# Retention attention into a routed MLP: where the sums, the weights and the placing of the early pair stand in the queues

## Chip, cores and metric

The kernel runs on one core of one Trainium2 chip. The metric is the time of one execution on the device in microseconds; the number compared is the median of several executions. All data are float32 unless said otherwise.

## The reference

An attention block without softmax (a retention: 4 batches, 8 heads, 768 positions, head width 64) gives 3072 rows of 512 numbers. Each row then goes through one of 8 experts, the one with the largest logit, and is scaled by its softmax probability.

```
state = gamma * state + k[t] (x) v[t];  y[t] = scale * q[t] @ state        # per batch and head
x = y of all heads side by side                                            # 3072 x 512
logits = x @ w_gate;  e = argmax(logits);  gate = softmax(logits)[e]
out[row] = gate * (relu(x[row] @ w1[e]) @ w2[e])                           # w1: 512 x 1024, w2: 1024 x 512
```

## The kernel before, in words

**Attention.** The work is cut into 12 steps (`STEPS`), each of two tiles of 128 rows. Step s computes the scores of a block of positions, the part that comes from the running state, the new state and the outputs (`scores`, `with_state`, `next_state`, `within`). One step later, `to_rows` turns the outputs into rows on VectorE and `store` writes them to a buffer in device memory, `x_d`, by four DMAs on SyncE's queue; `logits` and `logits_of` give the gate logits.

**Routing while attention runs.** Rows are sorted to experts in three portions (`NEXT` = 0, 5, 9, 12), by the generator `place(i)`. Each `next(rest)` issues its next piece: softmax parts and the chosen expert, then the ranks (small matmuls `rk`, then VectorE up to `here`), then `found` (a matmul), then the addition to `inv` (line 705), the table from which rows are fetched and written back. `WHEN` and `step` (764 to 768) say in which step and at which of five places ("p", "a", "b", "r", "c") a piece is issued. At the end of portion 1, GpSimd gathers the first 256 rows of expert 0 and of expert 1 from `x_d` by indirect DMAs (the early rows). Portion 2, of the last six tiles, is placed after the steps.

**The early pair.** Expert 0's first 256 rows, two tiles of 128, are computed before the other rows are known. In the last step ScalarE copies them (`xe`), TensorE transposes them (`early_rows`), and the loop at 840 runs the first layer over 8 f-blocks of 128 (`layer1`, `hTa`), with the pieces of portion 2 between the blocks. The second layer of the pair is done in `pair` by Winograd's scheme with seven products of half matrices in place of eight. It needs four sums of w2's quarters (`halves_of_w`, tiles `we`) and four of `hTa`'s (`halves_of_h`, tiles `he`). The products come in the order A11 B11; S2 T2; S3 T3; S1 T1; A12 B21; A22 T4; S4 B22. Between them stand VectorE's parts (`part`, line 361) and 16 transposes of expert 0's other rows into `xTa` (`spare`).

**Sums and queues.** Before, VectorE makes sums 0 and 1 of w2, sums 0 and 1 of h and sum 3 of w2; GpSimd makes sum 2 of w2 and sums 2 and 3 of h. `arms` (line 429) works out from the row counts which of 33 code variants each expert takes, and `regs` (414) loads that number into registers of TensorE and ScalarE. `sources`, `gates_of` and `targets` (179 to 208) are short chains of VectorE operations on `inv`: where rows come from, their gate and where they go. The late gathers of 128-row tiles 2 and 3 of both experts follow `sources`.

**Weights.** `weights1` and `weights2` issue DMAs on SyncE's queue, in program order with the stores. Expert 0's w1 comes in step 9 in two halves; half of its w2 (1 MB) is asked for after the store of step 10's rows, the other half after that of step 11's.

**After the pair.** Jobs of the 8 experts follow, with 512 rows at most each; job 0 does what is left of expert 0 and begins at once with `layer1` on `xTa`.

**Order.** From line 739 on, the order on all five engines is that of the program text (`manual_schedule`); nothing is reordered. An instruction that waits holds up all behind it on its engine or queue.

Of the kernel before, what the change touches and what calls it, by code (L numbers as in the profile page):

```python
# [13 lines left out]
F32 = mybir.dt.float32  # L14
# [4 lines left out]
ALU = mybir.AluOpType  # L19
AX = mybir.AxisListType  # L20

P = 128
# [31 lines left out]
def kernel(  # L54
# [11 lines left out]
    nc = tc.nc  # L66
# [87 lines left out]
            nc.sync.dma_start(w1t[:, :, :, part], w1v[:, ds(e, 1), :, part])  # L154
        return w1t

    def weights2(pool, e, part=range(FT), w2t=None):
        if w2t is None:
            w2t = pool.tile([P, 1, FT, DM], F32, tag="w2t", name="w2t")
        part = slice(part.start, part.stop)  # L160
        nc.sync.dma_start(w2t[:, :, part, :], w2v[:, ds(e, 1), part, :])
        return w2t

    def weights(pool, e):
# [86 lines left out]

    FH, DH = FT // 2, DM // 2

    def halves_of_h(hT, hs, others=nc.vector):


        hs = [h.rearrange("p (f t) -> p f t", f=FH) for h in hs]
        a11, a12, a21, a22 = (hT[:, ts(j, FH), ts(i, P)] for i in range(2) for j in range(2))
        nc.vector.tensor_tensor(out=hs[0], in0=a21, in1=a22, op=ALU.add)
        nc.vector.tensor_tensor(out=hs[1], in0=hs[0], in1=a11, op=ALU.subtract)  # L260
        others.tensor_tensor(out=hs[2], in0=a11, in1=a21, op=ALU.subtract)
        others.tensor_tensor(out=hs[3], in0=a12, in1=hs[1], op=ALU.subtract)
        return hs

    def halves_of_w(w2t, ws, which=range(4), by=nc.vector):
# [176 lines left out]
    with ExitStack() as actx:  # L442
# [145 lines left out]
        def store(s):  # L588
            m, b1, e = where[s]
            xg = x.pop(("g", s))  # L590
            for g in range(Q):
                nc.sync.dma_start(x_d[ts((2 * m + e) * 2 + b1, 2 * P), ts(g, P)].rearrange("(t l) r -> l t r", l=L),
                                  xg[ts(g, L), :, :, :].rearrange("p b q r -> p (b q) r"))
# [14 lines left out]
        def logits_of(s, lgT, bank):  # L608
            tr = bank[:, 2 * P : 4 * P].rearrange("p (b t) -> p b t", b=2)
            for b in range(2):  # L610
                nc.tensor.transpose(tr[:, b, :], lgT[:, ts(b, P)], ident)
            return lambda: nc.vector.tensor_reduce(
                lg[:, 2 * s : 2 * s + 2, :], tr.rearrange("p b (a e) -> p b e a", a=DT)[:, :, 0:E, :], axis=AX.X,
                op=ALU.add)
# [146 lines left out]
                copy(out=xTa[:, :, ts(t, P)], in_=tr)  # L761

        rest = iter(())
        WHEN = {5: "abc", 6: "ab", 7: "ab", 8: "pp", 9: "ar", 10: "pp"}

        def step(s, at):
            for _ in range(WHEN.get(s, "").count(at)):
                next(rest, None)

        for s in range(STEPS):  # L770
            if s + 3 < STEPS:
                if s % 2:
                    load_all("q", s + 3)
                load_all("k", s + 3)
                load_all("v", s + 3)
            if s % 2 and s + 1 < STEPS:
                scale_q(s + 1, 1)
            if s + 1 < STEPS:
                for b in range(2):
                    scale_v(s + 1, b)  # L780
            if s % 2 == 0 and s + 2 < STEPS:
                scale_q(s + 2, 0)
            if s in (1, 2):
                nc.gpsimd.memset(xs2[s % 2], 0.0)
            if s:
                am = [scores(s, b) for b in range(2)]
            y = outputs()
            if s + 1 == STEPS:
                logit = logits(s - 1)
            if where[s][0] or where[s][2]:  # L790
                with_state(s, y)

            def ahead():
                for b in range(2):
                    turn_k(s + 1, b)

            def ahead_q():
                if s % 2:
                    for b in range(2):
                        turn_q(s + 1, b)  # L800

            step(s, "p")
            if s:
                if s + 1 < STEPS:
                    logit = logits(s - 1)
                    ahead()
                if s + 1 == STEPS:
                    for t in range(HALF):
                        nc.scalar.copy(out=xe[:, t, :].rearrange("p (a q l) -> p q a l", q=Q, l=L),
                                       in_=xs2[0][:, t, :].rearrange("p (q a l) -> p q a l", q=Q, l=L))  # L810
                reduce = logits_of(s - 1, *logit)
                if s + 1 < STEPS:
                    ahead_q()
                to_rows(s - 1)
                reduce()
                store(s - 1)
                if s == NEXT[NR - 1]:
                    wa = [weights1(first, 0, 2)]
                if s + 1 == STEPS:
                    wa.append(weights2(first, 0, range(FT // 2)))  # L820
                if s in NEXT:
                    rest = chain(rest, place(NEXT.index(s) - 1))
                step(s, "a")
            next_state(s)
            step(s, "b")
            if s == NEXT[NR - 1] + 1:
                pad_ranks(acc[:, NR - 1, 0:2])
            step(s, "r")
            within(s, y, am, early_rows if s + 1 == STEPS else lambda: None)
            if s == 0:  # L830
                ahead()
            step(s, "c")

        rest = place(NR - 1)
        oa = xs2[0][:, 0:HALF, :]
        we = [att.tile([P, FH * DH], F32, tag=tag, name="we", bufs=bufs)
# [3 lines left out]
        for f in range(FT):  # L840
            layer1(EARLY, xTa, wa[0], hTa, f, (("sc", 4),))
            if f == 0:
                logit = logits(STEPS - 1)
            if f == 1:
                logits_of(STEPS - 1, *logit)()
                next(rest)
                to_rows(STEPS - 1)
                store(STEPS - 1)
                weights2(first, 0, range(FT // 2, FT), wa[1])
            if f == 3:  # L850
                next(rest)
            if f == 4:
                ne = count()
            if f == 6:
                next(rest)
                next(rest, None)
        src, far = sources(inv, "")
        for e in range(2):
            gather(xs2[e], src[:, ts(e, TC)], range(HALF, TC))
        egates, gates = gates_of(early[0], "_e"), gates_of(inv, "")  # L860
        arm, over = arms(ne)
        dst = targets(inv, far, "")
        halves_of_w(wa[1], we, [0, 1])
        halves_of_w(wa[1], we, [2], nc.gpsimd)
        S = halves_of_h(hTa, [att.tile([P, FH * P], F32, tag="k", name="he", bufs=8) for _ in range(4)], nc.gpsimd)
        T = halves_of_w(wa[1], we, [3])
        which = regs(0)

        late = turns(xs2[0], xTa, range(HALF, TC))

        def some(n):
            for _ in range(n):
# [2 lines left out]
        pair(hTa, wa[1], S, T, oa, egates, lambda: fetch_ahead(which, 0),  # L875
             lambda name: att.tile([P, FH * P], F32, tag="v", name=name, bufs=8)[:, 0:DH], some,
             (("sc", 4), ("sc", 4), ("y", 2), ("y", 2)))
        scatter(oa, targets(*early, "_e"), range(HALF))
        turn(xs2[1], xT1, range(TC))
        cols = [(src[:, ts(e, TC)], dst[:, ts(e, TC)], gates[:, ts(e, TC)]) for e in range(E)]  # L880

        cols[0] = (None, dst[:, HALF:TC], gates[:, HALF:TC])
# [204 lines left out]
```

## Time and profile before

| What | us |
|---|---|
| median of 3 runs | 462.06 |
| the runs | 461.9 to 463.61 |
| the profiled execution | 460.4 |
| its span on the chip | 458.7 |
| busy TensorE (PE) | 432.3 |
| busy VectorE (DVE) | 278.8 |
| busy GpSimd (POOL) | 249.1 |
| busy ScalarE (ACT) | 126.1 |
| mean granted TensorE clock | 0.985 |

The profiled execution is one run; its span is what the instructions on the chip cover, and the 1.7 us between the two lie around it. Places in the span are given in microseconds from its start. Attention's steps run to about 119, the first layer of the early pair to about 135, its second layer to about 157, and the jobs of the experts to 450. In the page, PE is a matmul and PEld the load of its weights, which overlaps; SPq is SyncE's queue of DMAs. A line number such as L271 is that of the kernel, and of a helper where one issues the instruction. "<-" names who ended a wait.

### The profile page before, as it was taken

What the parts mean: (1) busy time and instruction counts of PE and PEld (TensorE: products, weight loads), DVE (VectorE), ACT (ScalarE), POOL (GpSimd) and SP (SyncE); (2) the same over time, 40 slices, a digit from 0 to 9 for tenths busy, and PEclk for the clock granted to TensorE, in tenths of its full rate; (3) what the DMA queues carried; (4) which work ended last, traced back from release to release, by engine and by line L of the source; (5) the groups of instructions that cost most, each with busy time, mean ns of one, the idle gap of its engine ahead of it and who ended that gap; (6) DMA issues with size and microseconds to landing.
All of it is one profiled execution on the core that took longest, in us unless ns stands there. A gap on an engine that the chain in (4) does not pass through costs nothing.

```text
span 458.7 us, 9508 instructions
## 1 busy us (share of the span) xinstructions
PE 432.3 (94%) x3595; PEld 352.8 (77%) x3595; DVE 278.8 (61%) x583; ACT 126.1 (27%) x286; POOL 249.1 (54%) x203
## 2 busy tenths in 40 slices
PE   7799999988985999999999999999999999999992
PEld 4688888876764855669968995897897699699772
DVE  4444689696377984643775677267666848744410
ACT  3355355343410111120231131124132112202310
POOL 4575535445026058548906890984589099089211
PEclk9999999999995999999999999999999999999998
DMA  9999999999750099425614713281481524001001
GB/s 201 234 236 211 238 242 215 236 203 301 228 156 25 25 378 385 164 98 199 213 33 160 258 72 137 78 299 36 159 260 58 186 92 172 6 6 64 4 29 50
DMA packets 94471, 72.75 MB, mean 159 GB/s; under 512 B 53898, under 2 KB 78474, under 8 KB 94352
## 3 DMA queue, kind: packets, MB, share of 16 engines
q1 hardware_dynamic: 89088, 58.74, 46.5%
q0 software_dynamic: 5120, 12.60, 7.6%
q8 instruction: 47, 0.77, 0.7%
q14 instruction: 72, 0.59, 0.4%
q10 hardware_dynamic: 144, 0.05, 0.0%
HBM read 60.88 MB, written 14.68 MB: 165 GB/s over the span
## 4 chain that ended last, share of the span: by engine, by line
PE 82%; DVE 7%; SPq 4%; DMA 3%; issue 2%; ACT 1%; POOL 0%; POOLq 0%; DVEq 0%; ACTq 0%
PE p L309 24%; PE p L355 18%; PE p L242 15%; PE p L229 6%; PE sc L523 3%; PE y L574 3%; PE hp L229 3%; SPq L472 2%; PE new L556 2%; PE trk L491 2%; PE y L543 2%; PE trq L491 2%; DMA xs<-x_d,src_e 1%; DMA k<-in_k_dram 1%; DVE xTa L215 1%
## 5 line engine op out<-in xcount | busy, mean ns | idle before, releaser
L242 PE MATMUL p<-w2t,hT 128*8 128x128 f32 (+6 forms) x496 | 67.3, 362 | 0.1
L242 PEld LDWEIGHTS p<-w2t,hT 128*8 128x8 f32 (+6 forms) x496 | 32.1, 122 | 31.0 <-issue 26.7
L215 DVE STREAM_TRANSPOSE xT<-xs 32x512 f32<-32x512 f32 x64 | 44.9, 702 | 6.2 <-issue 5.0
L400 POOL DMA_INDIRECT out_dram<-o,dst x30 | 29.8, 993 | 28.6 <-ACT o L250 12.1
L525 DVE TENSOR_TENSOR am<-sc,causal 128x512 f32<-128x512 f32 x48 | 30.1, 684 | 22.4 <-PE sc L523 20.8
L485 POOL TENSOR_TENSOR vs<-v,dec 128x512 f32<-128x512 f32 x23 | 23.6, 1043 | 32.0 <-DMA v<-in_v_dram 26.9
L215 DVE STREAM_TRANSPOSE xTs<-xs 32x512 f32<-32x512 f32 x48 | 33.7, 702 | 11.6 <-DMA xs<-x_d,src 7.5
L1046 POOL COPY turn_of<-t 128x1 f32<-128x1 f32 x6 | 1.1, 183 | 71.7 <-DVE t L295 71.7
L172 POOL DMA_INDIRECT xs<-x_d,src x28 | 28.3, 1012 | 18.8 <-issue 7.9
L355 PE MATMUL p<-ws,hs 128*128 128x256 f32 x168 | 37.4, 379 | 0.0
L309 PE MATMUL p<-t,w1t 128*128 128x196 f32 (+5 forms) x192 | 35.9, 330 | 0.3 <-DVE q L313 0.3
L309 PE MATMUL p<-t,s 128*128 128x196 f32 (+5 forms) x192 | 35.8, 329 | 0.0
L313 DVE TENSOR_TENSOR hT<-p,q 128x196 f32<-128x196 f32 (+5 forms) x72 | 23.8, 359 | 19.0 <-PE p L309 16.5
L355 PEld LDWEIGHTS p<-ws,hs 128*128 128x128 f32 x168 | 31.9, 190 | 4.3
L271 POOL TENSOR_TENSOR ws<-w2t,ws 128x1024 f32<-128x1024 f32 x14 | 33.0, 2357 | 0.6
L271 POOL TENSOR_TENSOR ws<-w2t 128x1024 f32<-128x1024 f32 x14 | 33.1, 2362 | 0.1
L309 PEld LDWEIGHTS p<-t,w1t 128*128 128x128 f32 x192 | 32.4, 190 | 0.7 <-DVE q L313 0.7
L309 PEld LDWEIGHTS p<-t,s 128*128 128x128 f32 x192 | 32.4, 190 | 0.0
L480 POOL TENSOR_TENSOR qs<-q,dec 128x512 f32<-128x512 f32 x22 | 22.3, 1042 | 17.2 <-DMA q<-in_q_dram 17.2
L361 DVE SCALAR_TENSOR_TENSOR o<-p,gate,q 128x256 f32<-128x256 f32 x21 | 10.1, 483 | 31.0 <-PE p L355 23.7
L313 DVE TENSOR_TENSOR q<-p,q 128x196 f32<-128x196 f32 (+5 forms) x48 | 16.4, 360 | 18.0 <-PE p L309 12.3
L523 PE MATMUL sc<-qT,kT 64*128 64x128 f32 x384 | 24.9, 279 | 2.3 <-ACT kT L510 2.3
(208 smaller groups left out, 825.8 us busy)
## 6 DMA issues: line engine op xcount, KB each, us to landing
w1t<-in_moe_w_dram SPq DMA_DIRECT2D x7, 2048.0 KB, 8.3
w2t<-in_moe_w_dram SPq DMA_DIRECT2D x7, 2048.0 KB, 10.5
k<-in_k_dram SPq DMA_DIRECT2D x24, 256.0 KB, 6.0
v<-in_v_dram SPq DMA_DIRECT2D x24, 256.0 KB, 5.4
x_d<-xg SPq DMA_DIRECT2D x48, 128.0 KB, 4.0
q<-in_q_dram SPq DMA_DIRECT2D x11, 512.0 KB, 6.1
w1t<-in_moe_w_dram SPq DMA_DIRECT2D x2, 1024.0 KB
w2t<-in_moe_w_dram SPq DMA_DIRECT2D x2, 1024.0 KB
```

Of the source, the lines that this page charges most:

```text
L172: nc.gpsimd.indirect_dma_start(out=xs[:, t, :], out_offset=None, in_=x_d[0:rows, :], in_offset=bass.IndirectOffsetOnAxis(ap=idx[:, t : t + ...
L215: nc.vector.transpose(xT[ts(g, L), :, 0 : n * P].rearrange("p a (t r i) -> p r t a i", r=Q, i=L)[:, r, :, :, :], xs[ts(r, L), tiles[0] : t ...
L229: nc.tensor.matmul(hp, lhsT=w1t[:, 0, dt, ts(f, P)], rhs=xT[:, dt, 0:n], start=(dt == 0), stop=(dt == DT - 1))
L242: nc.tensor.matmul(y[j * z : j * z + m, 0:c], lhsT=hT[:, f, t * P + r0 : t * P + r0 + m], rhs=w2t[:, 0, f, ts(j, c)], start=(i == 0), stop ...
L271: by.tensor_tensor(out=ws[i], in0=sums[i][0], in1=sums[i][1], op=ALU.subtract)
L309: nc.tensor.matmul(rows(y), lhsT=a(d, f), rhs=b(d), start=start and d == 0, stop=d == 1, skip_group_check=True)
L313: nc.vector.tensor_tensor(out=to, in0=rows(y), in1=rows(plus), op=ALU.add)
L355: nc.tensor.matmul(y, lhsT=a[:, f, :], rhs=b[:, f, :], start=start and f == 0, stop=f == FH - 1, skip_group_check=True)
L400: done = nc.gpsimd.indirect_dma_start(out=out[:, :], out_offset=bass.IndirectOffsetOnAxis(ap=idx[:, t : t + 1], axis=0), in_=o[:, t, :], i ...
L485: by.tensor_tensor(out=vs, in0=raw.pop(("v", s, b)), op=ALU.mult, in1=inner(dec[:, ts(NC + 2 * where[s][0] + where[s][2], H)], D))
L523: nc.tensor.matmul(sc[j][:, a, :], lhsT=kT[r, a, :], rhs=qT[r, a, :], start=True, stop=True)
L525: nc.vector.tensor_tensor(out=am[j], in0=sc[j], in1=middle(causal[:, :], HP), op=ALU.mult)
```

## The change

`halves_of_h` takes a list of sums in place of an engine, and all eight sums of the early pair are issued on VectorE, in the order w 0, w 1, h 0, h 1, w 2, h 2, w 3, h 3. Both halves of expert 0's w2 are asked for in the last step ahead of the store of step 10's rows. `arms` moves from behind the loop to f-block 4; the last pieces of portion 2, with `sources`, the late gathers and the gates of all rows, move from f-block 6 and behind the loop to f-block 5; `regs(0)` moves to f-block 6. The gates and targets of the early rows are worked out ahead of the loop, the targets of all rows behind the transposes of expert 1's rows. In the steps, place "p" moves from ahead of the logits to behind them and the key transposes (this concerns steps 8 and 10), and the ranks of portion 1 in step 9 move from place "r", ahead of `within`, to "c", behind it.

```diff
--- before.py
+++ after.py
@@ -154,11 +154,10 @@
             nc.sync.dma_start(w1t[:, :, :, part], w1v[:, ds(e, 1), :, part])
         return w1t
 
-    def weights2(pool, e, part=range(FT), w2t=None):
-        if w2t is None:
-            w2t = pool.tile([P, 1, FT, DM], F32, tag="w2t", name="w2t")
-        part = slice(part.start, part.stop)
-        nc.sync.dma_start(w2t[:, :, part, :], w2v[:, ds(e, 1), part, :])
+    def weights2(pool, e, parts=1):
+        w2t = pool.tile([P, 1, FT, DM], F32, tag="w2t", name="w2t")
+        for part in (ts(i, FT // parts) for i in range(parts)):
+            nc.sync.dma_start(w2t[:, :, part, :], w2v[:, ds(e, 1), part, :])
         return w2t
 
     def weights(pool, e):
@@ -251,15 +250,14 @@
 
     FH, DH = FT // 2, DM // 2
 
-    def halves_of_h(hT, hs, others=nc.vector):
+    def halves_of_h(hT, hs, which=range(4)):
 
 
         hs = [h.rearrange("p (f t) -> p f t", f=FH) for h in hs]
         a11, a12, a21, a22 = (hT[:, ts(j, FH), ts(i, P)] for i in range(2) for j in range(2))
-        nc.vector.tensor_tensor(out=hs[0], in0=a21, in1=a22, op=ALU.add)
-        nc.vector.tensor_tensor(out=hs[1], in0=hs[0], in1=a11, op=ALU.subtract)
-        others.tensor_tensor(out=hs[2], in0=a11, in1=a21, op=ALU.subtract)
-        others.tensor_tensor(out=hs[3], in0=a12, in1=hs[1], op=ALU.subtract)
+        sums = (a21, a22, ALU.add), (hs[0], a11, ALU.subtract), (a11, a21, ALU.subtract), (a12, hs[1], ALU.subtract)
+        for i in which:
+            nc.vector.tensor_tensor(out=hs[i], in0=sums[i][0], in1=sums[i][1], op=sums[i][2])
         return hs
 
     def halves_of_w(w2t, ws, which=range(4), by=nc.vector):
@@ -761,7 +759,7 @@
                 copy(out=xTa[:, :, ts(t, P)], in_=tr)
 
         rest = iter(())
-        WHEN = {5: "abc", 6: "ab", 7: "ab", 8: "pp", 9: "ar", 10: "pp"}
+        WHEN = {5: "abc", 6: "ab", 7: "ab", 8: "pp", 9: "ac", 10: "pp"}
 
         def step(s, at):
             for _ in range(WHEN.get(s, "").count(at)):
@@ -799,7 +797,6 @@
                     for b in range(2):
                         turn_q(s + 1, b)
 
-            step(s, "p")
             if s:
                 if s + 1 < STEPS:
                     logit = logits(s - 1)
@@ -809,15 +806,16 @@
                         nc.scalar.copy(out=xe[:, t, :].rearrange("p (a q l) -> p q a l", q=Q, l=L),
                                        in_=xs2[0][:, t, :].rearrange("p (q a l) -> p q a l", q=Q, l=L))
                 reduce = logits_of(s - 1, *logit)
+                step(s, "p")
                 if s + 1 < STEPS:
                     ahead_q()
                 to_rows(s - 1)
                 reduce()
+                if s + 1 == STEPS:
+                    wa.append(weights2(first, 0, 2))
                 store(s - 1)
                 if s == NEXT[NR - 1]:
                     wa = [weights1(first, 0, 2)]
-                if s + 1 == STEPS:
-                    wa.append(weights2(first, 0, range(FT // 2)))
                 if s in NEXT:
                     rest = chain(rest, place(NEXT.index(s) - 1))
                 step(s, "a")
@@ -831,6 +829,7 @@
                 ahead()
             step(s, "c")
 
+        egates, edst = gates_of(early[0], "_e"), targets(*early, "_e")
         rest = place(NR - 1)
         oa = xs2[0][:, 0:HALF, :]
         we = [att.tile([P, FH * DH], F32, tag=tag, name="we", bufs=bufs)
@@ -846,25 +845,27 @@
                 next(rest)
                 to_rows(STEPS - 1)
                 store(STEPS - 1)
-                weights2(first, 0, range(FT // 2, FT), wa[1])
             if f == 3:
                 next(rest)
             if f == 4:
                 ne = count()
-            if f == 6:
+                arm, over = arms(ne)
+            if f == 5:
                 next(rest)
                 next(rest, None)
-        src, far = sources(inv, "")
-        for e in range(2):
-            gather(xs2[e], src[:, ts(e, TC)], range(HALF, TC))
-        egates, gates = gates_of(early[0], "_e"), gates_of(inv, "")
-        arm, over = arms(ne)
-        dst = targets(inv, far, "")
+                src, far = sources(inv, "")
+                for e in range(2):
+                    gather(xs2[e], src[:, ts(e, TC)], range(HALF, TC))
+                gates = gates_of(inv, "")
+            if f == 6:
+                which = regs(0)
+        hs = [att.tile([P, FH * P], F32, tag="k", name="he", bufs=8) for _ in range(4)]
         halves_of_w(wa[1], we, [0, 1])
-        halves_of_w(wa[1], we, [2], nc.gpsimd)
-        S = halves_of_h(hTa, [att.tile([P, FH * P], F32, tag="k", name="he", bufs=8) for _ in range(4)], nc.gpsimd)
+        halves_of_h(hTa, hs, [0, 1])
+        halves_of_w(wa[1], we, [2])
+        halves_of_h(hTa, hs, [2])
         T = halves_of_w(wa[1], we, [3])
-        which = regs(0)
+        S = halves_of_h(hTa, hs, [3])
 
         late = turns(xs2[0], xTa, range(HALF, TC))
 
@@ -875,8 +876,9 @@
         pair(hTa, wa[1], S, T, oa, egates, lambda: fetch_ahead(which, 0),
              lambda name: att.tile([P, FH * P], F32, tag="v", name=name, bufs=8)[:, 0:DH], some,
              (("sc", 4), ("sc", 4), ("y", 2), ("y", 2)))
-        scatter(oa, targets(*early, "_e"), range(HALF))
+        scatter(oa, edst, range(HALF))
         turn(xs2[1], xT1, range(TC))
+        dst = targets(inv, far, "")
         cols = [(src[:, ts(e, TC)], dst[:, ts(e, TC)], gates[:, ts(e, TC)]) for e in range(E)]
 
         cols[0] = (None, dst[:, HALF:TC], gates[:, HALF:TC])
```

## The prediction

> **What bounds the kernel now.** I read the granted clock and the page first: PE is busy 94% of the span at a mean clock of 0.985, and the chain of work that ended last is 82% PE. A gain therefore has to come from a stretch where PE does not run. I cut the span into stretches by busy time per engine. After 157 us PE is busy without a break (20.00 of 20.00 us at 180 to 200 and at 200 to 220), and the hole is just before it:
>
> ```profile
> 134.70:144.20 9.50, 2.65 (x8) 1.73 (x9) 9.15 (x20) 1.21 (x3) 7.89 (x6) 0.66 0.19 51
> 144.20:157.30 13.10, 12.74 (x49) 10.37 (x49) 9.86 (x22) 0.47 (x1) 2.11 (x1) 0.85 0.01 3
> ```
>
> The columns are the stretch, its length, busy PE, PEld, DVE, ACT, POOL, then the granted clock, the DMA share and GB/s. In the first stretch PE works 2.65 us of 9.50 and DVE 9.15. A clock of 0.66 and 0.85 means (1-0.66) x 2 x 9.5 + (1-0.85) x 2 x 13.1 = 10.4 us at half clock. The chain names DVE for the whole hole:
>
> ```profile
> 128.91 3.56 PE hp L229 x16
> 132.47 0.43 PE found L701 x6
> 132.92 0.33 DVE inv L705
> ...
> 135.45 0.17 DVE arm L435
> ...
> 137.20 1.22 DVE we L271
> 138.44 1.22 DVE we L271
> 139.66 2.76 DVE he L259
> 142.44 1.65 DVE he L260
> 144.22 3.77 PE yp L355 x8
> ...
> 157.29 7.36 PE p L229 x64
> ```
>
> The reader should see a row of small DVE operations from 132.92, then two sums of w2 and two of hTa, and only then the second product of the early pair. The two he sums took 2.83 and 1.63 us; the same shape in job 1 (hs L259 to L262) takes 0.69. Beside them stood POOL's sums, in the timeline of POOL and in the waits:
>
> ```profile
> 139.38 2.49 POOL L271 TENSOR_TENSOR we<-w2t 128x1024 f32<-128x1024 f32 x1
> 141.82 1.71 POOL L261 TENSOR_TENSOR he<-hTa 128x512 f32<-128x512 f32 x1
> 144.22 2.11 POOL L262 TENSOR_TENSOR he<-hTa,he 128x512 f32<-128x512 f32 x1 [0.69 <-DVE he L260]
> ...
> PE yp L355 <- DVE he L260: 4.9, 1, 4.9
> PE yp L355 <- DVE bt L196: 2.0, 1, 2.0
> ```
>
> The 2.0 us wait is the register load of the arm: it began on PE at 135.66, just after arm L435, and the first product followed 1.03 us later. The third view is SP's queue, for the weights and the rows:
>
> ```profile
> 107.46 11.15 SPq L592 DMA_DIRECT2D x_d<-xg  x8
> 118.65 0.48 SPq L161 DMA_DIRECT2D w2t<-in_moe_w_dram  x1
> 127.08 1.83 SPq L592 DMA_DIRECT2D x_d<-xg  x4
> 128.95 0.48 SPq L161 DMA_DIRECT2D w2t<-in_moe_w_dram  x1
> ```
>
> **What the Trainium skill says.** "SBUF — State Buffer", section "Who interferes with whom": a VectorE instruction with two SBUF inputs contends with a GpSimd instruction that reads SBUF, and the one that issued second blocks. The trace agrees: he L259 lost 2.14 us and L260 0.94 us beside POOL's sums. The same place infers that descriptor generation for GpSimd's DMAs is not hit by such sums; the trace agrees too (we L271 took 1.21 us beside the gathers of 137.05 and 138.35). "TensorE: Matmul & The Clock Gate", section "What's actually happening": the clock halves after an idle window of about 3.4 us, with free-running windows. The trace shows about three such windows at half clock after the holes of 2.03 and 4.89 us, and none after a hole of 1.47 us at 97.67. "DMA: Bandwidth & Descriptors", section "Queues, rings and completion order": one issuing queue is served in ring order, different queues take turns. The trace agrees in part: see the w2 step.
>
> **The change, part by part.** *The sums.* POOL's three go (2.49, 1.71, 2.11 us) and the stretch of 2.14 + 0.94 us on DVE with them; DVE gets one more sum of w2 (1.22) and two of hTa (0.69 each), all eight ahead of the pair's parts.
>
> *Arms one f-block earlier.* Six operations, 134.64 to 135.87, so 1.25 us; they now follow the count, which ended on DVE at 130.92, and end at 132.17. *Placing one block earlier.* `found` moves from after f-block 6 to after block 5, which ends at 130.6, but it needs the last `here` (130.85): PE waits 0.3 us. It ends near 131.4, so inv L705 starts at 132.17 behind the arms, not at 132.92. *Register loads after block 6.* Bounds: 1.03 us on PE as at 135.66, or nothing, as at 155.05, where the load ran 0.32 us while seven matmuls were still queued. The arm is ready before block 6 has run (131.4 to 133.1); I take zero. On ACT the load stands between two relus that wait 1.3 us for PE.
>
> *Targets moved.* The eight of the early rows and two gates go ahead of the loop, where DVE idles 6.08 us; the eight for all rows (135.79 to 137.27, 1.3 us once overlap with the arms is taken off) go behind the transposes of xT1. Their user, the scatter of job 0, is issued at 172.99 and waits on ACT's output at 172.3; the transposes end near 163. Zero.
>
> *DVE's chain, summed.* From 130.92: arms 1.25, inv 0.33, sources 0.85 (132.5 to 133.35; four gathers start on POOL 1 us earlier than 134.39), gates 0.35, four sums of w2 at 1.23 = 4.92, four of hTa at 0.68 = 2.72. That is 10.4 us, to 141.35. Block 7's relu is ready at 135.4, ahead of the first hTa sum (136.2). The first part u L361 started at 148.10 before, so DVE is **6.75 us** ahead. From there to the first matmul of job 0 was 157.29 - 148.10 = 9.19 us, with 16 transposes and four parts back to back on DVE. Nothing of it changes: job 0 starts at 150.5.
>
> *Is PE then later than DVE?* First product 135.0 to 136.7; second after he L260, at 137.7, a hole of 0.95 us; at full clock 1.73 each, so its result is there at 139.6, and DVE reads it only at 141.35. That 1.7 us covers PE; if the cover is gone, each us more is lost. The last product waits for the fourth part (148.1), a new hole of 1.8 us.
>
> *w2 ahead of the rows.* SP issues two halves (0.48 us each) right behind the store of step 9, near 111 instead of 118.65 and 128.95. What it is moved past: the four stores of step 10 (issued from 115.97) now stand behind 2 MB, about 6.3 us at the 330 KB/us of w1; they land near 124.5. Only the late gathers read them (133.5), and step 11's four stores are issued at 127.08 as before. What could suffer is POOL's own queue: the first two early gathers, issued at 108.36 and 109.92, landed at 115.3 and 116.4, and ACT's xe, the transposes and f-block 0 (118.8) hang on them. The trace shows that a weight transfer in flight delays a gather's first packets (issued 108.36, first packets 112.8, against 1.9 us for the one of 134.39), and that both then run side by side (at 303 to 305, 225 KB/us for the gather against 170 for w2). Their rows move while step 9's store is still on SP's ring, so w2 meets only the tail of the second: I take 0.2 us, bounds 0 and 6.3.
>
> *Steps 8 and 10, `found` behind the key transposes.* inv comes about 1.6 us later on DVE. In step 10 the gather follows, but POOL stood until 107.34 for the store of step 8 to land and issued at 108.36; the new index is ready near 107.9. In step 9 the ranking goes behind the outputs: PE loses its wait of 1.47 us, DVE gets the ranks 0.4 us later. Both end at the same gather. I take 0.1 us of loss for all, bounds 1 us of loss and 0.3 of gain. If the store landed earlier, that cover would be gone and 1.6 us lost.
>
> *After 157.* w1 of expert 1 was issued at 158.18, when the last parts released the memory; it, the transposes of xT1 and all else move with them, so the gain is kept. **Sum:** 6.75 - 0.3 (w2 and steps 8 to 10) = 6.4 us. The profiled execution took 460.4 us with a span of 458.7; it would take 454.0. The median of the runs, 462.06, is 1.7 us above it; on it the forecast is 455.6.
>
> **The rivals.** (1) *The clock.* The new 1.8 us hole, and 0.6 us before job 0, halve the clock for a window: the last product and the start of job 0 lose about 2 us, giving 457.6. For: 2.03 us preceded a drop. Against: 1.47 us did not. (2) *Early gathers partly behind w2*: 1 to 4 us, giving about 458. (3) *Slower: the early gathers' rows wait for the whole of w2.* Place: xe at 116.47. Price: 2 MB at 330 KB/us and the landing, 7.1 us, and PE idle so long that the clock halves as it did at 137.8, about 3 us; less 6.4 gives 465.7. It decides from a delay of 6.4 us. Against: gather packets ran beside weights elsewhere. (4) *The sums do not shorten*: each of the three that run beside gathers (133.5 to 138.5) is held as L259 was, 3 x 2.14 = 6.4 us, giving 462. Against: we L271 was not.
>
> **Chances.** Likeliest 0.62 (own range 453.5 to 457.2, from the unknown ends of the register load, steps 8 to 10 and the runs' own spread of 1.7 us), clock 0.16, partial delay 0.09, behind w2 0.05, no shortening 0.08. A difference of 0.5% (2.3 us) is about what a measurement of this kernel can tell from no change. Faster takes the likeliest, the clock and two thirds of the partial delay; slower is rival 3. The range leaves out rivals 3 and 4 and a little of each end.
>
> **What would show it.** Right: he L259 and L260 at 0.69, no POOL sum of `we`, the second product near 138 at full clock, job 0's first matmul near 150.7, block 0 still near 119. Wrong: xe later than 117.5, he sums over 1 us, a half clock after 146, or PE idle at the register load between blocks 6 and 7.

## The result, and the profile after

The kernel with the change took **456.32 us** (median of 19 runs, 453.64 to 465.75) against 462.26 us (19 runs) for the kernel before beside it, a gain of 5.9 us between the medians. The ratio is 0.9857 [0.9837, 0.9878]. Here and below a ratio is taken from the fast runs alone, those within 1.5% of the fastest of the same kernel: 17 of 19 here, but 13 of 22 in `e6` and 7 of 21 in `e8` further down. The forecast was 455.6 us, a gain of 6.4. That the total was right is partly luck: the sums, the placing and w2 were to bring 6.55 us and brought 7.7 to 8.9 between medians (`e1` and `f1` below), while the moves in the steps, priced at 0.1, cost 2 to 3.

The profiled execution took 457.6 us with a span of 455.9 us, 1.3 above its median; that of before was 1.9 below its own. So the two profiles lie only 2.8 us apart, and stages are compared by their lengths, not by places alone. In the lines below, numbers are the start in the span and the duration in us; lines stand two lower than before in this part of the code (L269 is the old L271, L353 the old L355, L359 the old L361).

First the chain of waits of the changed kernel:

```profile
126.64 3.46 PE hp L228 x16
131.90 1.16 DVE val L690
133.05 0.98 DVE here L681 x6
136.53 1.23 DVE we L269
...
143.12 0.69 DVE he L260
143.81 0.79 DVE u L359 x2
...
154.25 13.96 DMA w2t<-in_moe_w_dram
```

From 131.90 on VectorE alone leads to the first part. The sums follow each other with none of the 2.83 and 1.63 us of before, and the first part `u` comes right behind the last. The last line is new: in this profile job 1 waits for weights. The second view is the timeline of TensorE over the pair and the start of the jobs; brackets hold the idle time before a group and what ended it:

```profile
134.17 3.69 PE L228 MATMUL hp<-xTa,w1t 128*128 128x256 f32 x16
137.70 1.89 PE L353 MATMUL yp<-w2t,hTa 128*128 128x256 f32 x8
140.48 5.42 PE L353 MATMUL yp<-we,he 128*128 128x256 f32 x24 [0.88 <-DVE he L260]
...
150.52 1.99 PE L353 MATMUL yp<-w2t,he 128*128 128x256 f32 x8 [1.17 <-DVE xs L359]
152.91 7.36 PE L228 MATMUL p<-xTa,w1t 128*128 128x104 f32 x64 [0.39 <-DVE xTa L214]
...
168.20 2.21 PE L228 MATMUL p<-xT,w1t 128*128 128x392 f32 x6 [1.06 <-DMA w2t<-in_moe_w_dram]
```

F-blocks 6 and 7 run as one group of 16 matmuls, so the register load at 135.0 made no hole. The wait of 4.9 us before the second product is 0.88, and the one before the last product is 1.17. The stretches show the clock in the pair (columns as before: stretch, length, PE, PEld, DVE, ACT, POOL, clock, DMA share, GB/s):

```profile
137.87:143.70 5.83, 4.95 (x23) 4.03 (x23) 5.79 (x7) 1.22 (x3) 4.92 (x4) 1.00 0.25 59
143.70:152.90 9.20, 7.64 (x35) 6.08 (x34) 8.84 (x22) 0.47 (x1) 0.38 (x1) 1.00 0.08 23
```

The clock is full where it was 0.66 and 0.85; VectorE is busy 5.79 of 5.83 us and is the bound. Last, SyncE's queue:

```profile
113.77 2.53 SPq L590 DMA_DIRECT2D x_d<-xg  x4
116.35 1.54 SPq L160 DMA_DIRECT2D w2t<-in_moe_w_dram  x2
119.16 12.91 SPq L590 DMA_DIRECT2D x_d<-xg  x8
```

w2 is asked for ahead of step 10's stores, as meant, but at 116.4 and not near 111, since that step itself came later. This is where the lengths show the loss:

| us | before | after |
|---|---|---|
| block 0 of the early pair starts | 118.75 | 121.93 |
| from there to the end of the count | 12.17 | 12.18 |
| from the count to the first part `u` | 17.18 | 9.61 |
| from there to job 0 | 9.19 | 9.19 |
| job 0 to job 1 | 14.49 | 15.29 |
| half clock up to 440, at (length) | 137.8 (10.2) | 107.7 (3.4) |

The pair is 7.56 us shorter (38.54 to 30.98). Block 0, which was to stay near 119, is 3.2 us late, and a half clock has appeared at 107.7. How much of the 3.2 us the change made is worked out below.

### The profile page after: what moved, and what is told of

Its sections match the earlier page's. It is cut to its first block, busy times and chain, and to the rows that moved or that the text cites. A ratio compares the mean times of both kernels' runs of the same rounds, so it can differ in the third digit from the quotient of the medians.

```text
span 455.9 us, 9503 instructions
## 1 busy us (share of the span) xinstructions
PE 429.5 (94%) x3595; PEld 352.9 (77%) x3595; DVE 282.0 (62%) x586; ACT 127.8 (28%) x286; POOL 245.5 (54%) x200
## 4 chain that ended last, share of the span: by engine, by line
PE 76%; DMA 8%; DVE 6%; SPq 5%; issue 3%; ACT 1%; POOLq 0%; POOL 0%; ACTq 0%; DVEq 0%
PE p L307 25%; PE p L353 18%; PE p L241 13%; PE p L228 5%; DMA w2t<-in_moe_w_dram 3%; PE y L572 3%; DMA k<-in_k_dram 3%; PE sc L521 3%; SPq L470 2%; PE trq L489 2%; PE new L554 2%; PE hp L228 2%; PE trk L489 1%; DVE xTa L214 1%; DMA xs<-x_d,src_e 1%
## 5 line engine op out<-in xcount | busy, mean ns | idle before, releaser
L171 POOL DMA_INDIRECT xs<-x_d,src x28 | 31.0, 1107 | 18.6 <-issue 7.3
L353 PE MATMUL p<-ws,hs 128*128 128x256 f32 x168 | 37.4, 379 | 0.0
L353 PEld LDWEIGHTS p<-ws,hs 128*128 128x128 f32 x168 | 31.9, 190 | 4.3
L311 DVE TENSOR_TENSOR hT<-p,q 128x196 f32<-128x196 f32 (+5 forms) x72 | 24.8, 360 | 15.7 <-PE p L307 15.2
L269 POOL TENSOR_TENSOR ws<-w2t,ws 128x1024 f32<-128x1024 f32 x14 | 33.1, 2361 | 0.6
L269 POOL TENSOR_TENSOR ws<-w2t 128x1024 f32<-128x1024 f32 x14 | 33.1, 2364 | 0.2
L359 DVE SCALAR_TENSOR_TENSOR o<-p,gate,q 128x256 f32<-128x256 f32 x21 | 10.1, 483 | 31.3 <-PE p L353 30.9
L353 PE MATMUL p<-w2t,hT 128*128 128x256 f32 x112 | 27.0, 382 | 0.1
```

Source lines behind the costliest of these rows:

```text
L171: nc.gpsimd.indirect_dma_start(out=xs[:, t, :], out_offset=None, in_=x_d[0:rows, :], in_offset=bass.IndirectOffsetOnAxis(ap=idx[:, t : t + ...
L269: by.tensor_tensor(out=ws[i], in0=sums[i][0], in1=sums[i][1], op=ALU.subtract)
L311: nc.vector.tensor_tensor(out=to, in0=rows(y), in1=rows(plus), op=ALU.add)
L353: nc.tensor.matmul(y, lhsT=a[:, f, :], rhs=b[:, f, :], start=start and f == 0, stop=f == FH - 1, skip_group_check=True)
```

## The experiments

**Theory:** what was moved in steps 8 to 10 costs 2 to 3 us, which the forecast priced at 0.1; the sums and the placing bring more than 7 us. **Rivals:** w2 ahead of the rows delays block 0; or block 0 is late in this profile by chance. Four kernels were run beside each other on each of three chips; only runs on the same chip are subtracted from one another.

### The same kernel again, and the steps as before

`again` is the changed kernel without any edit. `e1_steps_back` undoes only the moves in the steps:

```diff
-        WHEN = {5: "abc", 6: "ab", 7: "ab", 8: "pp", 9: "ac", 10: "pp"}
+        WHEN = {5: "abc", 6: "ab", 7: "ab", 8: "pp", 9: "ar", 10: "pp"}
...
+            step(s, "p")
             if s:
...
                 reduce = logits_of(s - 1, *logit)
-                step(s, "p")
```

> The changed kernel itself once more, for a second profile beside the others. Two readings of the first one are to be told apart. (a) The 3.2 us by which f-block 0 began later (121.9 against 118.75) belong to that one execution: then block 0 is near 119 to 120 here. (b) They belong to the change: then block 0 is near 122 again, with a hole of several us on TensorE in step 10, `here` on VectorE stretched beside GpSimd's scaling of v, and a half-clock window near 108 to 111. The pair itself, from block 0 to job 0's first matmul, takes 31.0 us in both (38.5 before). Time 456 to 457 us, ratio 0.987.

> The changed kernel with the steps of attention as before: place p ahead of the logits again, and the ranks of step 9 ahead of the outputs. Theory 1 (the later found of step 10 exposes the early gather): block 0 begins 1.5 to 3 us earlier than in the changed kernel, time 454 to 455, ratio 0.982 to 0.984. Theory 2 (the gather waits for the store of step 8 anyway and the moves cost nothing): block 0 as in the changed kernel within 0.5 us, ratio 0.986 to 0.987. Theory 3 (taking away the 1.47 us wait for the ranks is worth something): slower than the changed kernel by 0.5 to 1.5 us, ratio 0.988 to 0.990.

`again`: 456.73 us, 0.9872 [0.9818, 0.9926], block 0 at 122.83, half clock at 107.9. `e1_steps_back`: 453.87 us, 0.9809 [0.9760, 0.9858], 2.86 us below `again`; block 0 at 119.63, no half clock before 445, and the pair still 30.98 us long. Every run of `again` (455.39 and up) is slower than every run of `e1` (455.14 and less). So the loss is no chance, though a part of the late block 0 is, as the count below shows; and it is not w2, which `e1` asks for at the same place in the queue: neither rival explains the loss. The time fits the first theory of `e1`; the reason that it gives, the later `found`, is not the one that the runs below show.

### The sums alone, the placing alone

`e2_sums_only` is the kernel before with the eight sums on VectorE; `e6_placing_only` is the kernel before with arms, pieces, sources, gathers, gates, registers and targets where the change puts them, and the sums as before, three of them on GpSimd.

The edit of `e2`:

```diff
-        halves_of_w(wa[1], we, [2], nc.gpsimd)
-        S = halves_of_h(hTa, [...], nc.gpsimd)
+        halves_of_h(hTa, hs, [0, 1])
+        halves_of_w(wa[1], we, [2])
+        halves_of_h(hTa, hs, [2])
         T = halves_of_w(wa[1], we, [3])
+        S = halves_of_h(hTa, hs, [3])
```

and the core of that of `e6`:

```diff
             if f == 4:
                 ne = count()
+                arm, over = arms(ne)
-            if f == 6:
+            if f == 5:
                 next(rest)
                 next(rest, None)
+                src, far = sources(inv, "")
...
+            if f == 6:
+                which = regs(0)
```

> The kernel before with nothing changed but the sums of the early pair: all eight on VectorE in the order of use. Theory 1 (the stretch of 3.1 us on VectorE beside GpSimd goes, and the three sums that come to it lie ahead of the first part): the two he sums at 0.69 us, the first part near 144.8 instead of 148.1, gain 3.3 us, ratio 0.993. Rival (the two sums were not what the first part waited for, or the half clock stays and takes the gain): gain under 1 us, ratio 0.998 to 1.000.

> The kernel before with only the placing moved: arms behind the count in f-block 4, the last pieces, sources, late gathers and gates in f-block 5, register loads in f-block 6, gates and targets of the early rows ahead of the loop, targets of all rows behind the transposes of xT1. The sums stay where they were, three of them on GpSimd. Theory 1 (the two halves of the sum add up): the first sum of w2 starts 3.4 us earlier and the gain is 3.4 us, ratio 0.9925. Rival (GpSimd's sums still come behind its four gathers, which move by 1 us alone, and the third product waits for them): gain 1 to 2 us, ratio 0.996 to 0.998. TensorE does not stop at the register load in either.

`e2`: 457.97 us, 0.9893 [0.9843, 0.9943], 4.8 us below the kernel before beside it; from block 0 to job 0 35.46 us, that is 3.08 less than before. `e6`: 461.70 us, 0.9922 [0.9894, 0.9951]; 33.80 us, 4.74 less. The runs of `e6` scatter from 455.7 to 468.8 for a reason that was not found: by its median it gains 1.1 us, by the ratio 3.6, so what the placing alone is worth in time stays open. In the length of the pair the two come to 7.82 us together, against the 7.56 of the whole, so there they add up almost fully. Both also shorten the half clock, from 10.2 us before to 6.8 in `e2` and 3.4 in `e6`. What then bounds `e6` is GpSimd's sum, as the timeline of its TensorE has it:

```profile
143.64 5.41 PE L355 MATMUL yp<-we,he 128*128 128x256 f32 x16 [2.50 <-POOL he L261]
```

The third product waits 2.50 us for a sum on GpSimd. On VectorE, the second sum of w2 also waited 0.31 us for the transfer of w2: asked for as before, w2 is only just there when the placing is earlier.

### The moves in the steps, alone and one at a time

`e7_steps_only` is the kernel before with both moves. `e5_ranks_late` and `f4_ranks_late_again` are the changed kernel with only "p" moved back, so that the ranks of step 9 stay behind the outputs; in `f3_found_late_only` only the ranks are moved back. `f1_steps_back_again` repeats `e1` beside them.

The edit of `e5` and `f4`, on the changed kernel:

```diff
+            step(s, "p")
             if s:
...
                 reduce = logits_of(s - 1, *logit)
-                step(s, "p")
```

of `f3`, on the changed kernel:

```diff
-        WHEN = {5: "abc", 6: "ab", 7: "ab", 8: "pp", 9: "ac", 10: "pp"}
+        WHEN = {5: "abc", 6: "ab", 7: "ab", 8: "pp", 9: "ar", 10: "pp"}
```

and `e7` makes both edits the other way round, on the kernel before.

> The changed kernel with place p ahead of the logits again, and the ranks of step 9 left behind the outputs. So one half of the moves in the steps is undone. Theory 1 (the order of found in steps 8 and 10 is what costs, since VectorE's addition to inv then waits for it behind key transposes that run at half clock): inv of portion 1 follows the masks at once, block 0 begins 2 us or more earlier than in the changed kernel (near 120), time 454 to 455, ratio 0.981 to 0.984. Theory 2 (the ranks behind the outputs cost, by the later ranks and by one long hole of TensorE that halves the clock): it stays as in the changed kernel, 456 to 457, ratio 0.986 to 0.988. Half and half: 455.3.

> The kernel before with the moves in the steps alone: place p behind the logits and key transposes, the ranks of step 9 behind the outputs. Theory 1 (the moves cost 2.9 us whatever follows): ratio 1.005 to 1.007, block 0 near 122, a hole of near 4 us on TensorE in step 10 ahead of the logits. Theory 2 (they cost only beside the earlier w2 or the new pair): ratio 0.999 to 1.002.

> The changed kernel with the steps of attention as before, once more, as the measure for the three beside it on the same chip: ratio 0.981 as the first time; block 0 near 119.5, the pair 31.0 us.

> The other half of the moves undone: place p behind the logits and key transposes as in the changed kernel, the ranks of step 9 ahead of the outputs as before. Theory 1 (found behind the key transposes is the larger part of the cost): inv of portion 1 comes 1 us or more behind the masks, block 0 near 121, ratio 0.985 to 0.987, near the changed kernel's. Theory 2 (the ranks behind the outputs, which leave TensorE one long hole and the half clock after it, are the larger part): no half clock before 119, ratio 0.981 to 0.983.

> Place p as before, the ranks of step 9 behind the outputs as in the changed kernel, on the same chip as the other half and the steps-back kernel. The first time 0.9835 on another chip. Theory 1: ratio 0.981 to 0.983. Theory 2: 0.985 to 0.987, with a half clock between 104 and 112 as the first time.

| kernel | us | ratio to before | block 0 at | half clock, steps 9 to 11 |
|---|---|---|---|---|
| e5 (second chip) | 457.05 | 0.9835 [0.9783, 0.9886] | 120.75 | 104.5 for 6.8 |
| e7 (second chip) | 467.05 | 1.0043 [1.0019, 1.0067] | 124.64 | 107.8 and 118.0, 3.4 each |
| f1 (third chip) | 454.54 | 0.9837 [0.9801, 0.9873] | 119.67 | none |
| f3 (third chip) | 455.48 | 0.9843 [0.9814, 0.9872] | 118.74 | none |
| f4 (third chip) | 456.43 | 0.9887 [0.9852, 0.9922] | 121.43 | 105.7 for 6.8 |

Alone on the kernel before, the two moves **lose** 2.3 us (467.05 against 464.71 there), and the interval of the ratio lies above 1. Against `f1` on the same chip the ranks cost 1.9 us (`f4`) and `found` 0.9 (`f3`), but each difference is uncertain by about 2 us. On the second chip the ratio of `e5`, 0.9835, lies where its first theory put it, and its time, 457.05 us, where the second did; `e9` below, with the steps as before but w2 late, was no faster there (457.98). So the medians do not tell the two moves apart. A half clock between 104 and 119 stands in all five profiles with the ranks behind the outputs (the change, `again`, `e5`, `e7`, `f4`) and in none of the nine without.

The profiles do tell them apart. Block 0 scatters with the start of step 9: `ohs`, the operation of VectorE for which the ranks wait, starts anywhere from 97.06 to 100.39, with and without the moves. So block 0 is counted from `ohs`:

| ranks of step 9 | place "p" | kernels | us from `ohs` to block 0 |
|---|---|---|---|
| ahead of the outputs | as before | before, e1, e2, e6, e8, e9, f1, f2 | 20.57 to 21.37 |
| ahead of the outputs | moved | f3 | 21.31 |
| behind the outputs | as before | e5, f4 | 23.69, 22.48 |
| behind the outputs | moved | the change, again | 22.74, 22.44 |
| behind the outputs | moved | e7, on the kernel before | 25.72 |

Against 21.05, the mean of the nine in the first two rows, the ranks cost 1.4 to 2.6 us in the changed kernel (4.7 in `e7`, with a second half clock), and `found` behind the key transposes costs nothing that can be seen. The kernel before and `f3` started level (`ohs` at 97.38 and 97.43), and GpSimd's first early gather shows it, first before, then `f3`:

```profile
108.36 1.25 POOL L172 DMA_INDIRECT xs<-x_d,src_e  x1 [3.41 <-DVE pad L718]
108.34 1.24 POOL L171 DMA_INDIRECT xs<-x_d,src_e  x1 [3.94 <-DVE src_e L185]
```

Block 0 followed at 118.75 and 118.74. In its profile `f3` lost time only later: job 1 waited 2.21 us, and a half clock of 3.4 us began near 166.4. Of the 3.2 us by which block 0 of the change is later than that of before, 1.8 lie ahead of `ohs` (99.19 against 97.38), and 1.4 are the moves.

The mechanism can be read in three timelines. TensorE of the changed kernel in steps 9 and 10:

```profile
97.97 1.97 PE L572 MATMUL y<-am,vs 128*64 128x128 f32 x32
99.87 0.20 PE L655 MATMUL rk<-ohs,before 128*128 128x64 bf16 x1
...
107.19 0.65 PE L600 MATMUL parts<-xT,wg 128*32 128x256 f32 x8 [3.89 <-DVE am L523]
107.77 1.97 PE L489 MATMUL trk<-ident,k 128*128 128x128 f32 x8
109.53 0.63 PE L609 MATMUL parts<-ident,lgT 128*128 128x128 f32 x2
109.95 1.27 PE L699 MATMUL found<-val,here 128*128 128x160 bf16 x8
```

TensorE of `f1`, with the steps as before:

```profile
99.18 0.20 PE L655 MATMUL rk<-ohs,before 128*128 128x64 bf16 x1 [1.53 <-DVE ohs L634]
...
104.44 0.73 PE L699 MATMUL found<-val,here 128*128 128x160 bf16 x8
105.09 0.64 PE L600 MATMUL parts<-xT,wg 128*32 128x256 f32 x8
```

The wait of 1.5 us for `ohs` is gone, and TensorE is ahead for as long; but VectorE is the bound there, and at the next place TensorE waits 3.89 us for its masks `am`. Behind this wait the clock is half (107.7 to 111.1), and the key transposes, behind which `found` now stands, take 1.97 us, where they take 1.09 in `f3`. VectorE itself is late too, and the same two kernels show why. VectorE of the changed kernel:

```profile
99.19 0.23 DVE L634 TENSOR_TENSOR ohs<-em,idx 128x64 bf16<-128x64 f32 x1
...
103.44 3.09 DVE L681 TENSOR_SCALAR here<-rrow,prow 128x128 bf16<-128x128 bf16 x8
106.46 2.47 DVE L523 TENSOR_TENSOR am<-sc,causal 128x512 f32<-128x512 f32 x4
111.27 0.32 DVE L703 TENSOR_TENSOR inv<-inv,found 128x160 f32<-128x160 f32 x1 [2.34 <-PE found L699]
```

VectorE of `f1`:

```profile
98.90 0.22 DVE L634 TENSOR_TENSOR ohs<-em,idx 128x64 bf16<-128x64 f32 x1
...
102.79 1.39 DVE L681 TENSOR_SCALAR here<-rrow,prow 128x128 bf16<-128x128 bf16 x8
...
106.48 0.31 DVE L703 TENSOR_TENSOR inv<-inv,found 128x160 f32<-128x160 f32 x1
```

With the ranks behind the outputs, `here` starts 0.65 us later, of which 0.29 stood already at `ohs` and 0.36 are the move. GpSimd scales the values `v` from 104.28 for 2.04 us in the changed kernel and from 104.23 in `f1`: in `f1`, `here` has just ended (104.18), in the changed kernel it stands right beside it and takes 3.09 us, so the masks start 2.4 us later. Then `inv` waits 2.34 us for `found`. It starts 4.8 us after that of `f1`: 0.3 of it stood at `ohs`, 1.6 are hidden because `f1` waits longer for the store of step 8, 0.9 come back behind the gather, and 2.0 are left at block 0. In `f3`, with the ranks in their old place, `inv` waits only 0.97 us for `found`, and no clock falls in the steps. In `e5` and `f4`, where `found` stands as before, the row copies wait 0.2 us or nothing for the gather: there TensorE itself is late, by its half clock of 6.8 us.

A longer `here` alone does not do this. In `e6`, with the ranks in their old place, it met both products of GpSimd too (3.01 us), but TensorE had spent 1.42 us waiting for `ohs` long before, only 1.1 us of waits fell beside the longer `here` and the masks, the clock stayed full, and from `ohs` to block 0 it took 21.15 us.

### w2 as before

`e9_w2_as_before` and `f2_w2_as_before_again` are `e1` with the halves of w2 asked for behind the stores of steps 10 and 11.

```diff
-                if s + 1 == STEPS:
-                    wa.append(weights2(first, 0, 2))
                 store(s - 1)
+                if s + 1 == STEPS:
+                    wa.append(weights2(first, 0, range(FT // 2)))
...
                 store(STEPS - 1)
+                weights2(first, 0, range(FT // 2, FT), wa[1])
```

> The steps as before (as in e1), and w2 of expert 0 asked for as before: one half behind the store of step 10's rows, the other behind that of step 11's. Theory 1 (w2 ahead of the rows costs the early gathers nothing, and spares the second sum a wait of some tenths): time 453.9 to 454.5, 0 to 0.6 us slower than e1, ratio 0.981 to 0.983, a short wait for w2 ahead of the second sum. Rival (w2 in flight delays the early rows): faster than e1 by 0.5 us or more, xe earlier after its gather by as much.

> The steps as before, and w2 of expert 0 asked for as before. The first time it stood 0.46% higher than the steps-back kernel, but on another chip, while the pair took only 0.25 us longer. Theory 1 (w2 ahead of the rows is worth the wait of 0.28 us ahead of the second sum and no more): 0.2 to 0.5 us above the steps-back kernel, ratio 0.9815 to 0.982. Theory 2 (it is worth more, in the early rows or later): 1.5 us or more above it, ratio 0.984 or more.

`e9`: 457.98 us, 0.9855 [0.9810, 0.9900]. `f2`: 455.90 us, 0.9859 [0.9823, 0.9895], 1.36 us above `f1` on the same chip, between the two theories; the runs of the two overlap (451.76 to 456.90 in `f1`, 452.71 to 457.69 in `f2`), so this is not clear of the noise. `e9` was slower than either of its theories had it, on a chip where the kernel before was slower too. The pair took 31.23 and 31.38 us, against 30.98 and 30.97 with w2 ahead, with waits of 0.29 and 0.36 us for w2 ahead of the second sum. So asking for w2 earlier helps the pair by 0.3 to 0.4 us in the profiles; whether it brings more is open. It did not visibly delay the early gathers: from the issue of the second to its row copy it was 6.55, 6.60 and 6.06 us with w2 late (before, `e9`, `f2`), and 5.41, 6.51 and 6.32 with w2 ahead (the change, `e1`, `f1`).

### The last two sums on GpSimd

`e8_last_two_gpsimd` is `e1` with w sum 3 and h sum 3 on GpSimd, to shorten VectorE's chain (`halves_of_h` is given the engine as well).

```diff
-        T = halves_of_w(wa[1], we, [3])
-        S = halves_of_h(hTa, hs, [3])
+        T = halves_of_w(wa[1], we, [3], nc.gpsimd)
+        S = halves_of_h(hTa, hs, [3], nc.gpsimd)
```

> The steps as before (as in e1), and of the eight sums the last two (w 3 and h 3, which the sixth and the seventh product read) on GpSimd behind its four gathers; the other six on VectorE. Theory 1 (VectorE's row from the arms to the last transpose sets job 0's start, and these two are 1.9 us of it): the pair takes 29.1 to 29.6 us from block 0 to job 0 in place of 31.0, time 452 to 452.5, ratio 0.977 to 0.978. Rival (GpSimd comes to them too late, or stands in the way of VectorE's last two sums): 31 us or more, time 454 to 455.

The pair fell by 1.1 us, to 29.84, close to the 29.1 to 29.6 of the first theory. But the time does not show it: 461.54 us, with runs scattered from 453.2 to 464.8 and the profiled run the fastest of them. The ratio, 0.9818 [0.9786, 0.9851], is no better than that of `e1` (0.9809 and 0.9837). `e6` and `e8`, the two kernels that scatter so, are also the two that leave sums on GpSimd behind the new placing; whether that is the cause was not tested. In this profile the gain was lost again right behind the pair, in the timeline of TensorE:

```profile
164.98 21.31 PE L228 MATMUL p<-xT,w1t 128*128 128x392 f32 x64 [2.51 <-DMA w2t<-in_moe_w_dram]
```

Job 1 waits 2.51 us, where the changed kernel waits 1.06 and the kernel before 0.26; the profile names the transfer of w2 of expert 1, although the product itself reads w1. From job 0 to job 1 it is 14.49 us before, 15.05 in `e1`, 15.29 in the change, 16.74 in `e8`. This need not come of the shorter pair: the transfer was issued 1.34 us after the start of job 0 in the change and in `e8` alike (154.25 and 149.58), and `f3`, whose pair is not shorter, waited 2.21 us.

## Why the prediction was right, and where it was wrong

- **VectorE's chain, 6.75 us:** right in mechanism, 0.8 too small. From the count to the first part it took 9.61 us and not 10.43. Each sum took what was forecast (1.22 and 0.69 us), but most of them start 0.09 us before the one ahead ends, so the eight came to 7.19 us and not 7.64; arms were 1.0 us and not 1.25. From the first part to job 0 it is 9.19 us, exactly as taken over.
- **Register load at nothing:** right; no hole between f-blocks 6 and 7.
- **Holes of 0.95 and 1.8 us:** measured 0.88 and 1.17, both at full clock. Rival 1, a half clock after the new hole, fell.
- **w2 ahead, 0.2 us of loss:** the sign was wrong, as far as the profiles show. No delay of the early gathers stands out, and in the new placing a late w2 costs 0.3 to 0.4 us in the pair (`e9`, `f2`). Rivals 2 and 3, with w2 in the way of the gathers, fell.
- **Steps 8 to 10, "0.1 us of loss":** this is the step that failed. It measured 2.86 us in the run beside `again` and 2.3 on the kernel before; 1.4 to 1.7 us of it stand between `ohs` and block 0 in the two profiles of the changed kernel, and where the rest lies is open. Of the two moves in this term, `found` behind the key transposes was priced rightly: in `f3` its index was ready at 108.0, where the text had 107.9, and the gather came no later than before. The ranks behind the outputs were not. The text took TensorE's wait of 1.47 us as lost for good. But TensorE is not the bound there, and the wait came back as 3.89 us in one piece, with the clock halved behind it. And 0.4 us on VectorE was priced as 0.4 (it was 0.36), though it moved eight small operations under GpSimd's two products. In six of the nine kernels with the ranks ahead these operations were done, or all but done, when the products began (1.39 us); in all five with the ranks behind they met both (3.1 us). With both moves the cover was gone: GpSimd's queue had ended its wait for the store by 109.2, and the gather waited on for its index:

```profile
112.69 1.24 POOL L171 DMA_INDIRECT xs<-x_d,src_e  x1 [6.37 <-DVE src_e L185]
```

  The text had named this point ("If the store landed earlier, that cover would be gone and 1.6 us lost"), but what took the cover away was a later index and not an earlier store. One of its signs of being wrong, `xe` later than 117.5, came true with it (119.65).
- **"After 157 all else moves with it":** nearly. In this profile job 1 came 0.8 us later behind job 0, with w2 of expert 1 named; in `again` it was 0.6, with no transfer named.
- **The sums do not shorten (rival 4):** fell; `e2` alone saved 3.08 us of the pair.

The parts of the profiles add to -7.56 + 3.2 + 0.8, or -3.6 us, and a further 0.8 us was lost behind the start of job 1, so -2.8 us, the difference of the two profiles. The medians say -5.9. In the seven other kernels with the steps as before (`e1`, `e2`, `e6`, `e8`, `e9`, `f1`, `f2`) block 0 starts between 118.40 and 120.27, at 119.7 in the mean; the profile of before, at 118.75, was an early one. That accounts for about 1 of the 3.1 us between -2.8 and -5.9; where the rest lies is not settled.

The **best version** is `e1`, the change without its moves in the steps: 0.9809 [0.9760, 0.9858] and, on another chip, 0.9837 [0.9801, 0.9873], some 8 us below the kernel before and 2.9 below the changed kernel beside it.

## What to carry to other kernels

Before an idle wait is taken off an engine, ask whether that engine bounds the stage. If it does not, the wait moves to the next place where it meets the engine that does, and there it can join another: here 1.5 us became 3.9, and a half clock followed. Before operations are moved by even half a microsecond, look at what the neighbour engine does half a microsecond later. Where the start of a stage scatters from run to run, count its length from an operation ahead of what was moved: places in the span gave the moves 3.2 us here, and the count from `ohs` 1.4.

## What the runs showed of the hardware that was not expected

- **One-input operations on VectorE are held as well.** `here` is a tensor_scalar on bf16 with one tensor input: eight of them took 1.39 us alone and 3.09 us beside GpSimd's two-input products, which kept their 1.0 us each. With one product beside it, it was 2.18 (`e1`, `f3`). The Trainium skill, "SBUF — State Buffer", section "Who interferes with whom", names tensor_scalar among the operations that can contend with GpSimd; the forecast had used the section for two-input sums alone.
- **A gather issued under a VectorE sum takes longer on GpSimd.** The timeline of GpSimd in the changed kernel:

```profile
136.56 2.11 POOL L171 DMA_INDIRECT xs<-x_d,src  x1 [6.26 <-DVE gate L205]
138.97 1.50 POOL L171 DMA_INDIRECT xs<-x_d,src  x1 [0.30 <-issue]
```

  A sum of w2 had begun at 136.53, just before the first. In the kernel before, where no sum had begun ahead of a gather, they took 1.00 to 1.05 us, and in `e8` the fourth, issued after VectorE's sums had ended, took 1.00. The same section infers that such gathers are not hit by two-input sums; these lines speak against it for a gather that begins second. The starts alone do not decide it: in `f2` and `e6` the first gather also began 0.03 us behind the sum, and there it took 1.05 us and the sum 1.29. In the changed kernel the sums were not held (1.22 us), and the rows were not needed before 144.5, so it cost nothing here.
- **When the clock halves.** The waits of 0.88, 1.17 and 1.53 us left the clock full; 3.89 us in one piece halved it, and so did 2.3 us in four pieces within 4 us (`f4`, where TensorE took each `found` as it came). Between these it went both ways: a half clock of 3.4 us followed the 2.21 us before job 1 in `f3` and the 2.45 us there in `e5`, and none followed the 2.51 us in `e8`. That fits windows with edges of their own (the Trainium skill, "TensorE: Matmul & The Clock Gate", section "What's actually happening"), in which the same hole counts differently by its place; the runs don't show where the edges lie.
